# A fused attention and two-layer feed-forward kernel on one core: the second batch's attention result stored unsplit at first, reciprocals parted from their sums, six copies moved from ScalarE to VectorE

## The chip, the cores and the metric

The kernel runs on one core of a Trainium2 chip. The metric is the device time of one execution in microseconds (us). A core has TensorE (PE in the rows; PEld is its weight load), VectorE (DVE), ScalarE (ACT), GpSimd (POOL) and SyncE (SP, which here only starts transfers). Each of them works through its own list of instructions in order; an instruction whose input is not there yet holds up everything behind it on that engine. SBUF is the working memory, PSUM the memory that TensorE writes, in eight banks.

## What is computed

Windowed attention over 2 batches of 8 heads, 768 tokens and 64 features, then two feed-forward layers over all 1536 tokens (512 wide, 2048 hidden), all in float32:

```python
def _attn_ref(q, k, v, n_global, n_local):        # n_global 8, n_local 96
    scores = scale * np.matmul(q, k.transpose(0, 1, 3, 2)) + bias   # bias: -slope[h] * distance
    scores = np.where(keep, scores, -1e9)         # the first 8 keys, and the 96 keys up to the query
    a = np.exp(scores - np.max(scores, axis=-1, keepdims=True))
    a = a / (np.sum(a, axis=-1, keepdims=True) + 1e-09)
    return np.matmul(a, v)
...
x = attention, tokens by (heads * features)
h = x @ w_in;  g = h * np.tanh(log(1 + exp(h)));  x = g @ w_out          # layer 1
h = x @ w_in2; g = relu, or (h + 1) ** 2 / 4 where |h| < 1;  out = g @ w_out2   # layer 2
```

## The kernel before

**Split numbers.** TensorE multiplies in a reduced form of float32 (fp32r). Every operand of the feed-forward layers is therefore kept as two such numbers: a high part, a rounded copy (`rounded`), and a low part, the remainder (`remainder`, value minus high part). `split(hi, lo, src)` makes both, the copy on ScalarE and the subtraction on VectorE. The attention's result is `x_hi` and `x_lo`.

**Attention** is `attention_windows`. It has 24 steps s = 0 to 23: for each batch (0 to 11 the first, 12 to 23 the second) and each of four pairs of heads, t = s mod 3 counts three blocks of 256 queries. In a step, u is the half of the block and j the head of the pair. A step's work is spread over several turns of one loop, so that in turn s each engine gets, in this order:

- TensorE: the scores of step s + 1, the transposes ("turned probabilities") of step s - 2, the product with the values of step s - 3;
- VectorE: `softmax(s, 0)`, two custom instructions that take bias and minimum (L381); `normalise(s-1)`, which adds 1e-9 to the sums (L391, the "total"), takes reciprocals (L392) and leaves the multiplying to GpSimd (L396); the remainders `x_lo` of a finished block (L186); `softmax(s, 1)`; and `evict(s-2, 1)`, the copy of one half of the turned probabilities out of PSUM (tile `pts`, L183);
- ScalarE: the copy `x_hi` of a finished block (L181), the exponentials of step s (L386, each also adds up its row), and between the two pairs of them `evict(s-2, 0)`, the copy of the other half of `pts` (L181).

The scores have two pairs of PSUM banks, so the scores of step s + 1 wait until VectorE has read those of step s - 1; the transposes have one bank for each half, so the transposes of step s - 1 wait for both copies of step s - 2. Steps with t = 0 have 6 blocks of probabilities (copies of 128x384), the others 8 (128x512); the copies of a t = 0 step fall in a turn with t = 2. In turns with t = 2 and t = 0 a finished block of 512 and of 256 tokens is split. A table, `BESIDE`, adds work of the first feed-forward weights (their conversion on all three engines, names such as V00 or T10) and, from step 23 on, the first matmuls of layer 1.

**Layer 1** has steps n = 0 to 31, 16 pieces of the hidden layer for each batch; the second batch's `x_hi` and `x_lo` are read from step 16 on. In step n TensorE makes the hidden piece (L566, L567, L569: 24 matmuls of 384 columns), ScalarE and VectorE make its gate (`ff.gate`: L575 to L605) and convert weights for step n + 2 (among them L186 into `wlo`), and `ff.finish` puts the product with the output weights of step n - 1 on TensorE (L616). A hidden piece of step n + 1 goes into the banks that the gate of step n has to have read (L583). Layer 2 follows, with L625 and, later, L830 and L928 as its matmuls.

The order on every engine is the order in which the code is written: the arm with windows is entered under a manual schedule. The tiles of the weights are `whi` and `wlo`, one pair for each of 16 pieces; those of pieces 14 and 15 are first written late in layer 1.

Of the kernel before, what the change touches and what calls it, by code (L numbers as in the profile page):

```python
# [9 lines left out]
F32 = mybir.dt.float32  # L10
# [6 lines left out]
ALU = mybir.AluOpType  # L17
# [3 lines left out]
P = 128  # L21
# [6 lines left out]
FAR = 2.0 ** 40  # L28
EXP20 = 485165195.40979
PRE, NEAR = 2, 3  # L30

BIAS_ON = "vvappppv"
FIRST_ON = "ppvvvv"
# [14 lines left out]
def attention_then_two_ffn_kernel(  # L48
# [10 lines left out]
    nc = tc.nc  # L59
    B, NP, _, S = q.shape  # L60
    H, D = 2 * NP, P // 2
    NT, DM = out.shape
    NF = w1.shape[0]
# [14 lines left out]
    def half(j):  # L78
        return slice(j * D, (j + 1) * D)
# [48 lines left out]
    halves = [(half(c), slice(PW - c * HQ, P - c * HQ)) for c in range(2)]  # L128
# [35 lines left out]
    for rows, shared in halves:  # L164
        nc.vector.tensor_scalar(dist[rows, shared], rel[rows, shared], ng[rows], nl_far[rows],
                                op0=ALU.is_ge, op1=ALU.add)
# [12 lines left out]
    def rounded(on, to, src):  # L179
        if on == "a":  # L180
            nc.scalar.activation(to, src, AF.Copy)  # L181
        else:
            (nc.vector if on == "v" else nc.gpsimd).tensor_copy(to, src)  # L183

    def remainder(on, to, src, hi):
        (nc.vector if on == "v" else nc.gpsimd).tensor_tensor(to, src, hi.bitcast(F32), op=ALU.subtract)  # L186

    def split(hi, lo, src):
        rounded("a", hi, src)
        remainder("v", lo, src, hi)  # L190
# [122 lines left out]

    SC, TR, PV, HID = ((0, 1), (6, 7)), (2, 3), (4, 5), (6, 7)

    def attention_windows(x_hi, x_lo, bank, wts, opening):
        with ExitStack() as es:
            cp = es.enter_context(tc.tile_pool(name="a_const", bufs=1))
            rp = es.enter_context(tc.tile_pool(name="a_raw", bufs=3))
# [32 lines left out]
            steps = [(b, p, t) for b, p in pairs for t in range(NB // 2)]  # L352
            NU = len(steps)
# [15 lines left out]
                        if not i:  # L369
                            break  # L370

            def softmax(s, u):
                b, p, t = steps[s]
                if u == 0:
                    probs[s] = (prs[s % 3],
                                sp.tile([P, 2, 2, 4], F32, tag="st", name=f"st{s}", bufs=3))
                pr, st = probs[s]
                n = keys(2 * t + u)
                for j, ps in enumerate(scs[s]):
                    h = 2 * p + j  # L380
                    nc.vector.tensor_tensor_reduce(  # L381
                        pr[:, u, j, HQ:HQ + n], ps[:, u, 0:n], bias[:, h, near if n > P else own0],
                        scale=-scale, scalar=3e38, op0=ALU.add, op1=ALU.min,
                        accum_out=st[:, u, j, 0:1],
                    )
                    nc.scalar.activation(pr[:, u, j, HQ:HQ + n], pr[:, u, j, HQ:HQ + n], AF.Exp, scale=-1.0,  # L386
                                         bias=st[:, u, j, 0:1], accum_out=st[:, u, j, 1:2])

            def normalise(s):
                pr, st = probs[s]  # L390
                nc.vector.tensor_scalar(st[..., 2], st[..., 1], 1e-9, None, op0=ALU.add)  # L391
                nc.vector.reciprocal(st[..., 3], st[..., 2])  # L392
                for u in range(2):
                    n = keys(2 * steps[s][2] + u)
                    for j in range(2):
                        nc.gpsimd.tensor_scalar(pr[:, u, j, HQ:HQ + n], pr[:, u, j, HQ:HQ + n], st[:, u, j, 3:4], 1.0,  # L396
                                                op0=ALU.mult, op1=ALU.mult)
# [15 lines left out]
            def evict(s, c):  # L413
                n = len(blocks(s))
                dst, src = pts[s]
                rounded("av"[c], dst[:, 0:n, half(c)], src[c][:, 0:n])

            def values(s):
                b, p, t = steps[s]
                vr = vs[b, p]  # L420
                src = pts.pop(s)[0]
                place = {x: n for n, x in enumerate(blocks(s))}
                for u in range(2):
                    i = 2 * t + u
                    g, (t0, n) = [(g, x) for g, x in enumerate(pieces) if x[0] <= i * P < x[0] + x[1]][0]
                    pv = bank(PV[g], [n])
                    m = key_blocks(i)
                    for o in range(m):
                        for j in range(2):
                            nc.tensor.matmul(pv[half(j), i * P - t0:(i + 1) * P - t0], vr[:, 2 * i - m + 1 + o, j],  # L430
                                             src[:, place[u, j, o]], start=(o == 0), stop=(o == m - 1))
                    if (i + 1) * P == t0 + n:
                        done.append((x_hi[b][:, p, t0:t0 + n], x_lo[b][:, p, t0:t0 + n], pv))

            for h in range(2):
                bias_of(h)
            for s in range(-1, NU + 4):

                if s in (3, 7):
                    wts.load()  # L440
                if s >= 2 and s % 3 == 2 and s // 3 + 3 < len(pairs):
                    load_qk(rp, *pairs[s // 3 + 3])
                if s >= 6 and s % 3 == 0 and s // 3 + 1 < len(pairs):
                    vs[pairs[s // 3 + 1]] = load_v(rp, *pairs[s // 3 + 1])
                ready, done[:] = done[:], []
                for hi, lo, src in ready:
                    rounded("a", hi, src)
                if s + 1 < NU:
                    scores(s + 1)
                if 0 <= s - 2 < NU:  # L450
                    transposes(s - 2)
                if 0 <= s - 3 < NU:
                    values(s - 3)
                if 0 <= s < NU:
                    softmax(s, 0)
                if 0 <= s - 1 < NU:
                    normalise(s - 1)
                for hi, lo, src in ready:
                    remainder("v", lo, src, hi)
                if 0 <= s - 2 < NU:  # L460
                    evict(s - 2, 0)
                if 0 <= s < NU:
                    softmax(s, 1)
                if 0 <= s - 2 < NU:
                    evict(s - 2, 1)
                for name in BESIDE.get(s, ()):
                    opening[name]()
                    if name in ("V01", "V11"):
                        wts.load()


    def attention_all(x_hi, x_lo, bank, wts, opening):
        with ExitStack() as es:
            cp = es.enter_context(tc.tile_pool(name="b_const", bufs=1))
            rp = es.enter_context(tc.tile_pool(name="b_raw", bufs=2))
# [73 lines left out]
            for name in sum((BESIDE[s] for s in sorted(BESIDE)), ()):  # L549
                if name[0] != "b":  # L550
                    opening[name]()
                    if name in ("V01", "V11"):
                        wts.load()


    class FeedForward:
# [453 lines left out]
    def arm(attention, manual):  # L1010
        with ExitStack() as es:
# [26 lines left out]
            opening.update({f"h{n}{i}": lambda n=n: ff.hidden_piece(n) for n in range(2) for i in "ab"})  # L1038
            opening.update({f"g0{i}": lambda: ff.gate_part(0) for i in "abc"})
            batches = [slice(b * S, (b + 1) * S) for b in range(B)]  # L1040
            attention([x_hi[:, :, t] for t in batches], [x_lo[:, :, t] for t in batches], bank, wts, opening)
            wpb = es.enter_context(tc.tile_pool(name="wpb", bufs=1))

            due = {(B - 1) * NF + 2 + (3 * f // 2 if f < 10 else 2 * f - 5): (1, f) for f in range(NF)}

# [3 lines left out]
            def parts_of(n):  # L1049
                if n in due:  # L1050
                    m, f = due[n]
                    return wts.convert(wpa if f < NEAR else wpb, m, f)[1]
                if n + 1 >= NF:
                    return nothing, nothing, wts.finish
                if n + 2 < NF:
                    halves[n + 2] = wts.convert(wpb, 0, n + 2)[2]
                    first_half = halves[n + 2][0]
                else:
                    def first_half(second):
                        second()  # L1060
                _, begin, middle, high = halves[n + 1]
                if n > 1:
                    return begin, middle, lambda: first_half(high)

                def opens():
                    for name in ("R20", "H11", "R11"):
                        opening[name]()
                    begin()

                return opens, middle, lambda: first_half(high)  # L1070

            def again(f, dtype):
                pool = wpa if f < NEAR else wpb
                return [pool.tile([P, 2, DM], dtype, tag=f"w{n}{f}", name=f"w{n}{f}") for n in ("hi", "lo")]

            pair = Pair(x_hi, x_lo, bank, gp, tp, wts, again, dram, ff.finish)
            for n in range(1, ff.count):
                if n > 1:
                    ff.hidden(n)
                ff.gate(n, *parts_of(n))  # L1080
                ff.finish()
                for f in range(4, 12):
                    if n - 2 in due and due[n - 2] == (1, f):
                        pair.save(f)
                if n >= B * NF:
                    pair.beside(n - B * NF)
# [58 lines left out]
```

## Time and profile before

| | |
|---|---|
| median of 3 runs | 600.29 us (598.37 to 601.36) |
| the profiled execution's own time | 597.39 us |
| its span, first to last instruction | 595.6 us |
| TensorE busy | 582.7 us (98%) |
| VectorE busy | 460.0 us (77%) |
| ScalarE busy | 393.9 us (66%) |
| GpSimd busy | 65.2 us (11%) |
| mean granted TensorE clock | 0.999 |

Busy shares are means over the whole span. The attention fills about the first 65 us, layer 1 goes on to about 340 us, layer 2 to the end; each stretch has to be read by itself.

### The profile page before, as it was taken

The page shows a single profiled execution, that of the slowest core. Times are in us where ns is not written, and L with a number is a line of the kernel's source. Part 1 is how long each engine was busy: PE and PEld are TensorE (multiplying, and loading weights), DVE is VectorE, ACT ScalarE, POOL GpSimd, SP SyncE. Part 2 cuts the span into 40 slices and gives each one's busy share as a digit, 9 for nine tenths or more (in the row PEclk, how much of TensorE's full clock was granted, in tenths as well). Part 3 has the DMA queues.
Part 4 walks back from the last instruction along what each step waited for, and adds up shares of the span by engine and source line. Part 5 has one row for each costly group of instructions (what it writes and reads, how often), then busy time and mean ns, then how long its engine had stood idle before and what let it go on. Part 6 is the DMA issues. An engine that isn't in the chain of part 4 may idle for free.

```text
span 595.6 us, 10128 instructions
## 1 busy us (share of the span) xinstructions
PE 582.7 (98%) x3708; PEld 505.6 (85%) x3708; DVE 460.0 (77%) x1038; ACT 393.9 (66%) x872; POOL 65.2 (11%) x156
## 2 busy tenths in 40 slices
PE   5999999999999999999999999999999999999997
PEld 3767889999999999999999988878888888888886
DVE  7999889888888577676776775988788787777572
ACT  5999888888888468676686777577464643543240
POOL 5766600000000000000000000000020140200000
PEclk9999999999999999999999999999999999999999
DMA  7997032344333202241544665600042270310003
GB/s 205 307 297 249 4 134 95 124 142 142 120 103 132 71 1 72 71 142 52 161 139 145 186 205 175 180 32 2 0 137 76 68 216 1 107 36 1 0 18 130
DMA packets 17481, 66.66 MB, mean 112 GB/s; under 512 B 2192, under 2 KB 2704, under 8 KB 13328
## 3 DMA queue, kind: packets, MB, share of 16 engines
q1 hardware_dynamic: 11952, 56.11, 29.6%
q0 software_dynamic: 4608, 8.39, 5.0%
q10 hardware_dynamic: 864, 1.44, 0.6%
q8 instruction: 31, 0.51, 0.4%
q14 instruction: 26, 0.21, 0.1%
HBM read 54.40 MB, written 11.53 MB: 111 GB/s over the span
## 4 chain that ended last, share of the span: by engine, by line
PE 86%; DVE 6%; ACT 6%; issue 1%; POOL 0%; DVEq 0%; POOLq 0%; ACTq 0%
PE psum L616 22%; PE psum L928 15%; PE psum L830 13%; PE psum L566 10%; PE psum L567 10%; PE psum L569 10%; PE psum L625 7%; ACT pr L386 4%; DVE pr L381 1%; ACT pts L181 1%; DVE pts L183 1%; DVE x_lo L186 1%; ACT x_hi L181 0%; DVE wlo L186 0%; PE psum L430 0%
## 5 line engine op out<-in xcount | busy, mean ns | idle before, releaser
L566 PE MATMUL psum<-x_hi,whi 128*128 128x384 f32 (+1 forms) x320 | 111.2, 347 | 0.4 <-DVE kr L583 0.4
L567 PE MATMUL psum<-x_lo,whi 128*128 128x384 f32 (+1 forms) x320 | 110.5, 345 | 0.0
L616 PE MATMUL psum<-g_lo,whi 128*128 128x512 f32 (+1 forms) x256 | 86.7, 338 | 0.1
L616 PE MATMUL psum<-g_hi,wlo 128*128 128x512 f32 (+1 forms) x256 | 86.2, 337 | 0.0
L616 PE MATMUL psum<-g_hi,whi 128*128 128x512 f32 (+1 forms) x256 | 86.1, 336 | 0.0
L569 PE MATMUL psum<-x_hi,wlo 128*128 128x384 f32 (+1 forms) x320 | 71.8, 345 | 0.0
L566 PEld LDWEIGHTS psum<-x_hi,whi 128*128 128x128 f32 x320 | 60.2, 188 | 3.7 <-DVE kr L583 0.6
L181 ACT ACTIVATE whi<-wbits 128x512 fp32r<-128x512 f32 x72 | 44.6, 619 | 27.6 <-DVE wbits L783 14.1
L567 PEld LDWEIGHTS psum<-x_lo,whi 128*128 128x128 f32 x320 | 60.2, 188 | 2.4
L569 PEld LDWEIGHTS psum<-x_hi,wlo 128*128 128x128 f32 x320 | 57.3, 188 | 2.5
L186 DVE TENSOR_TENSOR wlo<-wbits,whi 128x512 fp32r<-128x512 f32 x76 | 51.9, 688 | 9.2 <-ACT whi L181 9.1
L756 POOL DMA_DIRECT2D whi<-kept_hi x16 | 8.7, 541 | 430.9 <-ACT room_lo L869 363.0
L616 PEld LDWEIGHTS psum<-g_lo,whi 128*128 128x128 f32 x256 | 48.2, 188 | 5.8 <-DVE g_lo L605 0.5
L616 PEld LDWEIGHTS psum<-g_hi,whi 128*128 128x128 f32 x256 | 48.2, 188 | 5.7
L616 PEld LDWEIGHTS psum<-g_hi,wlo 128*128 128x128 f32 x256 | 48.1, 188 | 5.7
L238 ACT ACTIVATE wbits<-stage 128x512 uint16<-128x512 uint16 x64 | 50.1, 783 | 0.3 <-DVE wlo L186 0.2
L386 ACT ACTIVATE pr<-pr,st 128x192 f32<-128x192 f32 (+1 forms) x96 | 41.9, 444 | 7.5 <-DVE st L381 7.4
L245 DVE SCALAR_TENSOR_TENSOR wbits<-wsc,wbits 128x512 uint32<-128x512 uint32 x60 | 41.5, 692 | 6.7 <-ACT wbits L238 2.5
L396 POOL TENSOR_SCALAR pr<-pr,st 128x192 f32<-128x192 f32 (+1 forms) x96 | 40.2, 437 | 20.6 <-ACT pr L386 8.2
L173 ACT ACTIVATE wsc<-stage 128x512 f32<-128x512 f32 x60 | 39.6, 660 | 0.0
L367 PE MATMUL psum<-kr,qr 64*64 64x192 f32 (+1 forms) x352 | 25.9, 360 | 8.0 <-DVE wsc L160 5.4
L575 ACT ACTIVATE e<-psum 128x384 f32<-128x384 f32 x32 | 15.5, 487 | 26.0 <-PE psum L569 25.9
(161 smaller groups left out, 1293.3 us busy)
## 6 DMA issues: line engine op xcount, KB each, us to landing
stage<-in_w_dram SPq DMA_DIRECT2D x32, 1024.0 KB, 5.0
vr<-in_v_dram SPq DMA_DIRECT2D x8, 704.0 KB, 10.7
kept_hi<-whi SPq DMA_DIRECT2D x8, 512.0 KB, 7.3
kept_lo<-wlo SPq DMA_DIRECT2D x8, 512.0 KB, 8.0
whi<-kept_hi POOLq DMA_DIRECT2D x16, 256.0 KB, 3.6
wlo<-kept_lo POOLq DMA_DIRECT2D x16, 256.0 KB, 3.7
kr<-in_k_dram SPq DMA_DIRECT2D x14, 216.0 KB, 12.0
qr<-in_q_dram SPq DMA_DIRECT2D x7, 384.0 KB, 11.2
```

The costliest lines, as they stand in the source:

```text
L181: nc.scalar.activation(to, src, AF.Copy)
L186: (nc.vector if on == "v" else nc.gpsimd).tensor_tensor(to, src, hi.bitcast(F32), op=ALU.subtract)
L238: nc.scalar.activation(bits[:, i, :, 0], words(U16, i, 1), AF.Copy, scale=2.0 ** -13, bias=2.0 ** -14 - 0.5)
L245: nc.vector.scalar_tensor_tensor(out[:, i].bitcast(U32), moved(i, U32), 3, out[:, i].bitcast(U32), op0=ALU.logical_shift_left, op1=ALU.bit ...
L386: nc.scalar.activation(pr[:, u, j, HQ:HQ + n], pr[:, u, j, HQ:HQ + n], AF.Exp, scale=-1.0, bias=st[:, u, j, 0:1], accum_out=st[:, u, j, 1:2])
L566: nc.tensor.matmul(ph, wh[:, c], xh[:, c, tok], start=(c == 0), stop=False)
L567: nc.tensor.matmul(ph, wh[:, c], xl[:, c, tok], start=False, stop=False)
L569: nc.tensor.matmul(ph, wl[:, c], xh[:, c, tok], start=False, stop=(c == KD - 1))
L616: nc.tensor.matmul(y, lhs[:, w], rhs[:, t0:t0 + n], start=(f == 0 and i == 0 and c % share == 0), stop=(f == NF - 1 and i == 2 and c % sha ...
L625: nc.tensor.matmul(ys[c], lhs[:, w], rhs, start=(f == 0 and i == 0), stop=(f == NF - 1 and i == 2))
L830: nc.tensor.matmul(ps, a[:, cols], x, start=(n == 0), stop=(n == 3 * HK - 1))
L928: nc.tensor.matmul(ys[c], lhs[:, w], rhs[:, cuts[c]], start=(n == 0 and k == 0), stop=(n == len(fs) - 1 and k == 2))
```

## The change

Three things are edited in `attention_windows`, and one follows in layer 1.

1. *Unsplit result.* For the second batch, a finished block is no longer split. Its 512 tokens are copied to a plain float32 place `raw_x` by ScalarE, its 256 tokens by VectorE. `raw_x` lies in the tiles of weight pieces 14 and 15, which for this come from a pool opened before the attention. The four splits (768 columns each) are done after the gates of layer 1's steps 5, 6, 7 and 8.
2. *Total and reciprocal parted.* `total(s-1)` stays where it was; `normalise(s-1)`, now only the reciprocal and GpSimd's multiplying, moves behind the first instruction of `softmax(s, 1)`, and the remainders move behind it.
3. *Six copies.* For t = 0 steps other than 6 and 9 (0, 3, 12, 15, 18, 21), `evict(s-2, 0)` is done by VectorE in place of ScalarE, and stands right behind the total.

```diff
-            def softmax(s, u):
+            def softmax(s, u, heads=(0, 1)):
...
+            def total(s):
+                st = probs[s][1]
+                nc.vector.tensor_scalar(st[..., 2], st[..., 1], 1e-9, None, op0=ALU.add)
+
             def normalise(s):
                 pr, st = probs[s]
-                nc.vector.tensor_scalar(st[..., 2], st[..., 1], 1e-9, None, op0=ALU.add)
                 nc.vector.reciprocal(st[..., 3], st[..., 2])
...
-                rounded("av"[c], dst[:, 0:n, half(c)], src[c][:, 0:n])
+                on = "v" if steps[s][2] == 0 and s not in (6, 9) else "av"[c]
+                rounded(on, dst[:, 0:n, half(c)], src[c][:, 0:n])
...
-                for hi, lo, src in ready:
-                    rounded("a", hi, src)
+                for g, to, src in ready:
+                    if g != 1:
+                        rounded("a", to[0], src)
...
                     softmax(s, 0)
                 if 0 <= s - 1 < NU:
+                    total(s - 1)
+                if 0 <= s < NU:
+                    if 0 <= s - 2 < NU:
+                        evict(s - 2, 0)
+                    softmax(s, 1, (0,))
+                if 0 <= s - 1 < NU:
                     normalise(s - 1)
-                for hi, lo, src in ready:
-                    remainder("v", lo, src, hi)
-                if 0 <= s - 2 < NU:
+                for g, to, src in ready:
+                    if g is None:
+                        remainder("v", to[1], src, to[0])
+                    elif g == 1:
+                        rounded("v", to[0], src)
+                if 0 <= s < NU:
+                    softmax(s, 1, (1,))
+                elif 0 <= s - 2 < NU:
                     evict(s - 2, 0)
-                if 0 <= s < NU:
-                    softmax(s, 1)
                 if 0 <= s - 2 < NU:
                     evict(s - 2, 1)
...
+        return [lambda p=p: split(x_hi[1][:, p], x_lo[1][:, p], raw_x[p]) for p in range(NP)]
...
                 ff.finish()
+                if n >= LATER and splits:          # LATER = 5
+                    splits.pop(0)()
```

On VectorE, turn 5 of the attention (t = 2) read so before, from the total of step 4 on (`st` holds the sums, ISA is the custom instruction of L381 and the reading of its minimum):

```order
L391 TENSOR_SCALAR st_371<-st_371 128x4
L392 RECIPROCAL st_371<-st_371 128x4
L186 TENSOR_TENSOR x_lo<-psum,x_hi 128x512
L381 ISA pr_190,st_422<-psum,bias 128x192
L381 ISA st_422 128x1
...
L183 COPY pts_401<-psum 128x6x64
```

and reads so in the changed kernel, whose line numbers are its own:

```order
L394 TENSOR_SCALAR st_375<-st_375 128x4
L184 COPY pts_405<-psum 128x6x64
L384 ISA pr_194,st_426<-psum,bias 128x192
L384 ISA st_426 128x1
L398 RECIPROCAL st_375<-st_375 128x4
L187 TENSOR_TENSOR x_lo<-psum,x_hi 128x512
...
L184 COPY pts_405<-psum 128x6x64
```

The first copy of `pts` now stands in front of the softmax of the second half-block, the reciprocal and the remainder behind one half of it; turns 2, 14, 17, 20 and 23 have the same shape, the last three without the remainder. The second place is VectorE in layer 1, between the gates of steps 5 and 6, before (`wlo_7` is weight conversion for step 7, `e` the gate of step 6):

```order
L242 TENSOR_SCALAR wbits<-stage_78 128x512
L245 SCALAR_TENSOR_TENSOR wbits<-wsc,wbits 128x512
L186 TENSOR_TENSOR wlo_7_1842<-wbits,whi_7_1841 128x512
L576 TENSOR_SCALAR e<-e 128x384
L577 SCALAR_TENSOR_TENSOR e<-e 128x384
```

and in the changed kernel:

```order
L243 TENSOR_SCALAR wbits<-stage_78 128x512
L246 SCALAR_TENSOR_TENSOR wbits<-wsc,wbits 128x512
L187 TENSOR_TENSOR wlo_7_1838<-wbits,whi_7_1837 128x512
L187 TENSOR_TENSOR x_lo<-whi_159,x_hi 128x768
L597 TENSOR_SCALAR e<-e 128x384
L598 SCALAR_TENSOR_TENSOR e<-e 128x384
```

One remainder of 768 columns has come in ahead of the next gate, and so it has ahead of the gates of steps 7, 8 and 9. On TensorE, GpSimd and SyncE every instruction stands where it stood.

## Rows read from the trace of the kernel before

**Rows 1.** Busy time by stretch: start:end, length, then busy us of each engine.
```profile
20.00:40.00 20.00, 19.27 (x346) 14.64 (x347) 18.97 (x95) 19.31 (x76) 13.60 (x34) 1.00 1.03 296
40.00:60.00 20.00, 19.05 (x325) 14.18 (x321) 19.42 (x91) 19.08 (x74) 12.98 (x31) 1.00 0.82 246
...
100.00:120.00 20.00, 20.00 (x118) 18.69 (x117) 17.46 (x35) 17.36 (x36) 0.00 (x0) 1.00 0.33 109
```

**Rows 2.** The chain that ended last, in order of time: start, length, what.
```profile
7.72 3.52 ACT pr L386 x16
...
66.26 1.02 PE psum L430 x16
```

**Rows 3.** Timeline of turn 20: start, length, instruction, [idle before <-releaser].
```profile
57.92 0.68 PE L411 MATMUL psum<-ident,pr 64*128 64x64 f32 x12
...
58.39 0.16 DVE L391 TENSOR_SCALAR st<-st 128x4 f32<-128x4 f32 x1
...
58.58 0.18 DVE L392 RECIPROCAL st<-st 128x4 f32<-128x4 f32 x1
...
58.68 0.66 DVE L186 TENSOR_TENSOR x_lo<-psum,x_hi 128x512 fp32r<-128x512 f32 x1
...
59.25 0.35 DVE L381 CUSTOM_DVE_ANT_0 pr<-psum,bias 128x192 f32<-128x192 f32 x1
...
59.80 0.55 DVE L183 COPY pts<-psum 128x384 f32<-128x384 f32 x1
...
60.27 0.28 DVE L381 CUSTOM_DVE_ANT_0 pr<-psum,bias 128x128 f32<-128x128 f32 x1
```

**Rows 4.** Timeline of turn 2 and the start of turn 3.
```profile
11.27 0.37 DVE L391 TENSOR_SCALAR st<-st 128x4 f32<-128x4 f32 x1 [0.28 <-ACT pr L386]
...
11.82 0.59 PE L411 MATMUL psum<-ident,pr 64*128 64x64 f32 x12
...
12.34 0.98 PE L367 MATMUL psum<-kr,qr 64*64 64x192 f32 x16
12.44 0.49 ACT L181 ACTIVATE pts<-psum 128x384 f32<-128x384 f32 x1
...
12.95 0.28 DVE L381 CUSTOM_DVE_ANT_0 pr<-psum,bias 128x128 f32<-128x128 f32 x1
```

**Rows 5.** Timeline of turn 5 and the start of turn 6.
```profile
18.28 0.17 DVE L391 TENSOR_SCALAR st<-st 128x4 f32<-128x4 f32 x1
...
18.32 0.59 PE L411 MATMUL psum<-ident,pr 64*128 64x64 f32 x12
...
19.86 0.51 PE L367 MATMUL psum<-kr,qr 64*64 64x192 f32 x4
```

**Rows 6.** Timeline of turn 21: a total beside a GpSimd instruction.
```profile
60.55 0.68 POOL L177 TENSOR_SCALAR stage<-stage 128x512 f32<-128x512 f32 x1
...
60.69 0.56 DVE L391 TENSOR_SCALAR st<-st 128x4 f32<-128x4 f32 x1
```

**Rows 7.** Timeline of the passage from attention to layer 1.
```profile
78.66 0.58 ACT L181 ACTIVATE x_hi<-psum 128x512 fp32r<-128x512 f32 x1
...
79.27 0.69 DVE L186 TENSOR_TENSOR x_lo<-psum,x_hi 128x512 fp32r<-128x512 f32 x1 [0.39 <-ACT x_hi L181]
...
85.60 0.44 PE L566 MATMUL psum<-x_hi,whi 128*128 128x384 f32 x1 [0.41 <-DVE kr L583]
```

**Rows 8.** Timeline of layer 1, from the end of gate 5 to the hidden piece of step 7.
```profile
122.21 0.69 DVE L186 TENSOR_TENSOR wlo<-wbits,whi 128x512 fp32r<-128x512 f32 x1 [0.70 <-ACT whi L181]
...
122.83 0.35 DVE L576 TENSOR_SCALAR e<-e 128x384 f32<-128x384 f32 x1
...
123.48 0.49 ACT L575 ACTIVATE e<-psum 128x384 f32<-128x384 f32 x1 [0.91 <-PE psum L569]
...
125.96 1.02 DVE L583 SCALAR_TENSOR_TENSOR e<-qr,psum 128x384 f32<-128x384 f32 x2
...
127.47 0.34 PE L566 MATMUL psum<-x_hi,whi 128*128 128x384 f32 x1
```

More of the change, by code (lines that the diff above doesn't have):

```diff
@@ L30 @@
 PRE, NEAR = 2, 3
+LATER = 5
 BIAS_ON = "vvappppv"
@@ L314, in attention_then_two_ffn_kernel, with attention_windows @@
     SC, TR, PV, HID = ((0, 1), (6, 7)), (2, 3), (4, 5), (6, 7)
-    def attention_windows(x_hi, x_lo, bank, wts, opening):
+    def attention_windows(x_hi, x_lo, bank, wts, opening, kept):
+        raw_x = [t.rearrange("p a n -> p (a n)")[:, 0:S] for f in (NF - 2, NF - 1) for t in kept(f, F32)]
         with ExitStack() as es:
@@ L370, in scores @@
                             break
-            def softmax(s, u):
+            def softmax(s, u, heads=(0, 1)):
                 b, p, t = steps[s]
-                if u == 0:
+                if (u, heads[0]) == (0, 0):
                     probs[s] = (prs[s % 3],
@@ L378, in softmax @@
                 n = keys(2 * t + u)
-                for j, ps in enumerate(scs[s]):
-                    h = 2 * p + j
+                for j in heads:
+                    ps, h = scs[s][j], 2 * p + j
                     nc.vector.tensor_tensor_reduce(
@@ L432, in values @@
                     if (i + 1) * P == t0 + n:
-                        done.append((x_hi[b][:, p, t0:t0 + n], x_lo[b][:, p, t0:t0 + n], pv))
+                        tok = slice(t0, t0 + n)
+                        done.append((g if b else None, (raw_x[p][:, tok],) if b else
+                                     (x_hi[b][:, p, tok], x_lo[b][:, p, tok]), pv))
             for h in range(2):
@@ L469, in attention_windows, with attention_all @@
                         wts.load()
-    def attention_all(x_hi, x_lo, bank, wts, opening):
+        return [lambda p=p: split(x_hi[1][:, p], x_lo[1][:, p], raw_x[p]) for p in range(NP)]
+    def attention_all(x_hi, x_lo, bank, wts, opening, kept):
         with ExitStack() as es:
@@ L553, in attention_all @@
                         wts.load()
+        return []
     class FeedForward:
@@ L1040, in arm, with again @@
             batches = [slice(b * S, (b + 1) * S) for b in range(B)]
-            attention([x_hi[:, :, t] for t in batches], [x_lo[:, :, t] for t in batches], bank, wts, opening)
+            pools = {f: wpa for f in (*range(NEAR), NF - 2, NF - 1)}
+            def again(f, dtype):
+                pool = pools[f]
+                return [pool.tile([P, 2, DM], dtype, tag=f"w{n}{f}", name=f"w{n}{f}") for n in ("hi", "lo")]
+            splits = attention([x_hi[:, :, t] for t in batches], [x_lo[:, :, t] for t in batches], bank, wts, opening,
+                               again)
             wpb = es.enter_context(tc.tile_pool(name="wpb", bufs=1))
+            pools.update({f: wpb for f in range(NF) if f not in pools})
             due = {(B - 1) * NF + 2 + (3 * f // 2 if f < 10 else 2 * f - 5): (1, f) for f in range(NF)}
@@ L1051, in parts_of @@
                     m, f = due[n]
-                    return wts.convert(wpa if f < NEAR else wpb, m, f)[1]
+                    return wts.convert(pools[f], m, f)[1]
                 if n + 1 >= NF:
@@ L1055, in parts_of @@
                 if n + 2 < NF:
-                    halves[n + 2] = wts.convert(wpb, 0, n + 2)[2]
+                    halves[n + 2] = wts.convert(pools[n + 2], 0, n + 2)[2]
                     first_half = halves[n + 2][0]
@@ L1070, in parts_of @@
                 return opens, middle, lambda: first_half(high)
-            def again(f, dtype):
-                pool = wpa if f < NEAR else wpb
-                return [pool.tile([P, 2, DM], dtype, tag=f"w{n}{f}", name=f"w{n}{f}") for n in ("hi", "lo")]
             pair = Pair(x_hi, x_lo, bank, gp, tp, wts, again, dram, ff.finish)
```

## The prediction

> **What bounds the kernel now.** First the busy time by stretch [rows 1], to see where the edits fall. Between 20 and 60 us, which is attention, TensorE, VectorE and ScalarE are each busy 19.0 to 19.4 of 20 us: three engines at their limit, none of which can make up more than about 5% of a delay. From 100 to 120 us TensorE is busy all of its 20.00 us while VectorE and ScalarE have 2.5 us of air in 20. The clock is 1.00 in all three stretches, so no edit is paid for or paid back by it. Second, the chain that ended last [rows 2]: it begins on ScalarE's exponentials at 7.72 and is on TensorE from 66.26 us to the end. So a microsecond by which attention hands over later, or earlier, is a microsecond of the result; and behind 66 us only what stops TensorE counts. Third, the timelines of single turns, since in attention the question is which wait ends last.
>
> **VectorE's list in attention.** Turn 20 [rows 3] gives the price of each piece as the distance from start to start, which is what a full engine pays: total to reciprocal 0.19 (58.39 to 58.58), reciprocal to remainder 0.10, remainder of 512 columns 0.57, first softmax piece of the second half-block with its minimum and the second of the same kind 0.55 together (59.25 to 59.80), copy of 384 columns 0.47. The total itself is written after 0.16 us, but the reciprocal behind it starts only 0.19 after it, and it must read what the total wrote; with softmax in between that wait has work in it. I put the parting at -0.1 per turn, between 0 and the whole 0.19.
>
> What the second batch loses: four remainders of 512 columns (0.57 each) become nothing on VectorE, since ScalarE makes the plain copy; four of 256 become copies of 256, at nothing gained or lost. What VectorE gains: six copies of 0.47. For turns 12 to 22 that is 11 x 0.1 + 3 x 0.57 less 3 x 0.47, or 1.4 us less work, and up to 2.0 if the totals that took 0.56 instead of 0.16 [rows 6] become short. ScalarE loses 0.49 per moved copy [rows 4]. By work alone the attention would gain 1.4 to 2.0.
>
> **What the moved copy waits for.** The copy reads transposes, and in VectorE's list it now stands ahead of three softmax pieces, of which TensorE's next scores wait.
>
> - Turn 2 [rows 4]. The total comes at 11.27, the transposes run from 11.82 to 12.41, and ScalarE's copy started at 12.44, the moment they ended. VectorE's copy can't start sooner: it waits about 0.8 us with the rest of its turn behind it. From 12.45: copy 0.47, softmax 0.28, reciprocal 0.10, softmax 0.28, second copy 0.47, so turn 3 begins at about 14.05 where it began at 12.95: +1.1. TensorE's next scores (12.34) need the second half-block read, at about 13.65: +1.3.
> - Turn 5 [rows 5]. TensorE is 1.3 late, so the transposes of 18.32 to 18.91 end at 20.2, while VectorE is ready some 0.3 to 0.8 earlier. From 20.2: copy 0.47, softmax 0.28, reciprocal 0.10, remainder 0.59, softmax 0.28, so the scores of 19.86 start at 22.0: +2.1. I take +2.1 for both turns. Below: if transposes keep pace, as in a turn where they are done before the total, the copy costs only its 0.47 on VectorE and gives 0.49 back on ScalarE: 0 for the two.
> - Turns 6 to 11 have no moved copy. All three engines are full [rows 1], so at most 5% of some 15 us comes back, 0.75; I take 0.2 from the parting.
> - Turns 14, 17, 20, 23. In turn 20 [rows 3] the transposes end at 58.60, the total at 58.55: with the lateness of both engines alike the copy waits almost nothing, but it and the remainder's place now stand ahead of softmax, and TensorE, as full as VectorE, gets its scores later in those turns. A walk in order through these turns with the pitches above gives back nearly all of the 1.4: I take -0.1, with the ends -2.0 (all of VectorE's saving arrives) and +1.0 (a wait of 0.25 in each of the four).
>
> Attention: 2.1 - 0.2 - 0.1 = **+1.8**.
>
> **The passage to layer 1** [rows 7]. The last block's copy of 512 columns on ScalarE (0.58) stays, its remainder on VectorE (0.69, after a wait of 0.39 for that copy) goes. TensorE waits 0.41 at 85.60 for VectorE. **-0.3**, between 0 and -0.41: more than the wait can't be gained there.
>
> **The splits in steps 5 to 8** [rows 8]. Each adds to ScalarE a copy of 768 columns, and to VectorE a remainder of 768. Neither stands in the trace. The copy: by 0.49 for 384 [rows 4] and 0.58 for 512 [rows 7] it is 0.76, at most 1.5 x 0.58 = 0.87; ScalarE has 0.91 of idle time ahead of 123.48, which hides it. The remainder: not under the 0.69 of 512 columns, not over 1.5 x 0.69 = 1.03; by the distance 122.21 to 122.83 it is 1.5 x 0.62 = 0.93, and I take 0.88. So VectorE has 0.88 x 4 = 3.5 us more, against 2.5 us of air in 20 us [rows 1], that is 1.05 in a step of 8.4: the room is there, but in four steps running nearly all of it is used up. Part of that air is the 0.70 for which VectorE waits at 122.21 for ScalarE, and that is moved with the rest rather than filled, since ScalarE in turn waits for VectorE's gate. The first split makes VectorE's L583 of 125.96 some 0.7 late; the bank's first half, read by 126.5, is needed at 127.47, about 0.95 away. Nothing is lost. The three behind it come on top of what the first left over: about 0.3, 0.55 and 0.55. **+1.4**; below it 0 (each step clears its own lateness), above it 2.8 (three splits arrive whole, at 0.93).
>
> **Sum.** 1.8 - 0.3 + 1.4 = +2.9 us. The profiled execution took 597.39, which would make 600.3; it lies 2.9 under the median shown, 600.29, and against that median the time is **603.2 us**. Half a per cent, 3.0 us, is about what a measurement of this kernel can tell from no change; the forecast lies just at that.
>
> **The rivals.**
>
> *Relief on ScalarE carries the attention* (faster). ScalarE starts the chain [rows 2], and loses six copies of 0.49. If the transposes run earlier because ScalarE's exponentials are done earlier, VectorE's copy finds them ready, turns 2 and 5 cost 0, and VectorE's 1.4 to 2.0 comes through. Then 600.29 - 1.7 - 0.3, with the splits at half my price (+0.7): 599.0; with the splits at 0, 598.3, and with ScalarE's relief of 6 x 0.49 on top at most 595.4. It decides if the wait ahead of the copy in turn 2 stays under about 0.3 us. For it: the chain's first link is ScalarE. Against it: at 11.27 VectorE was waiting 0.28 for ScalarE already, and TensorE's transposes began 0.55 behind that [rows 4]. I put this case at **597.8**.
>
> *GpSimd's multiplying meets the totals* (slower). In turn 21 a total of 4 columns took 0.56, starting 0.14 after a GpSimd instruction that ran from 60.55 to 61.23; it ended within 0.02 of that one [rows 6]. In turn 20 the same total took 0.16 [rows 3]. The parted reciprocal is 0.3 to 0.9 us later in its turn, so GpSimd's multiplying by it is later too, and falls on the next turn's total and copies more often. At 0.4 per meeting, and some six more meetings of 24 turns: +2.4, so 603.2 + 2.4 = **605.6**. It decides from about three more meetings on. Against it: the total in turn 5 was short, 0.17 [rows 5], as most are.
> On this the Trainium skill says, in "SBUF — State Buffer", "Who interferes with whom", that VectorE and GpSimd share one port pair under an exclusive lock, held for a whole instruction, the loser blocked. The 0.56 that ends with GpSimd's instruction agrees; by the rule VectorE's copies out of PSUM, with one output in SBUF and no second input there, would be blocked seldom, which speaks for fewer than six meetings.
>
> *The splits are hidden whole*: 603.2 - 1.4 = **601.8**. For it: 0.95 us of slack at the bank against 0.88 of work [rows 8]. Against it: the ring from VectorE to ScalarE and back carries lateness over.
>
> **How the numbers follow.** Forecast 0.42, from 601.7 to 604.7; ScalarE's relief 0.24, from 595.4 to 599; meetings 0.16, from 604.5 to 608; hidden splits 0.18, from 600.5 to 602.5. The limits of no change are 597.3 and 603.3. Faster: a little under half of the second case, 0.10. Slower: about half of the forecast and all of the third, 0.37. No change: the rest, 0.53. The range for 8 in 10 leaves out the far ends of the second and third case: 597.4 to 606.0. The forecast's own is 601.7 to 604.7.
>
> **What the changed profile would show.** VectorE idle before its copy of `pts` in turn 2, for some 0.8 us, released by TensorE's transposes, and turn 3 beginning near 14.05; idle again in turn 5, by 0.3 to 0.8; scores of turn 6 about 2 us late. The same copy in turns 14 to 23 with less than 0.3 of idle time. The first matmul of layer 1 about 1.8 late. No wait of VectorE for an `x_hi` of the second batch, and TensorE's 0.41 at gate 1 shorter. In layer 1 a step 5 as long as step 4, steps 6 to 8 longer by 0.3 to 0.6 with TensorE waiting for L583's successor, and from step 10 on the old length. A remainder of 768 of 0.8 to 1.0. Totals of 0.3 to 0.6 in more than six further turns would be the second rival's mark.
>
> **What would make it wrong.** Above all the turns 12 to 23, where I let waits eat 1.4 us of saved work on the strength of a walk by fixed prices: if TensorE has more air there than 5%, the saving arrives. Then the two waits at the start, whose 2.1 us stand on transposes that don't move: if they move up by 0.5, more than half of it goes. Last, the splits, whose price and whose leftover are both my estimates.

## The result and the profile after

The changed kernel takes **604.87 us** (median of 6 runs, 604.38 to 606.21), the kernel before 600.91 (6 runs, 598.37 to 601.84). The ratio is 1.0074, 95% interval 1.0047 to 1.0101: slower by half a per cent to one. The forecast was 603.2, its range 597.4 to 606.0. Against the kernel before that ran beside it the change costs 4.0 us by the medians, where the sum had 2.9; the likeliest of its three cases, no change (0.53, up to 603.3), did not come, but slower (0.37).

The profiled execution of the changed kernel has a span of 603.5 us, 7.9 more than the 595.6 of the one shown before, twice what the medians differ by. The first view is busy time by stretch (length, busy us of PE, PEld, DVE, ACT, POOL, then granted clock, DMA share, GB/s):

```profile
12.40:19.10 6.70, 5.79 (x64) 4.04 (x64) 4.12 (x22) 3.28 (x14) 3.67 (x9) 0.50 1.02 308
20.00:40.00 20.00, 19.63 (x341) 14.62 (x338) 16.75 (x85) 18.19 (x71) 13.85 (x34) 1.00 1.03 293
100.00:120.00 20.00, 20.00 (x117) 18.96 (x116) 17.01 (x34) 17.30 (x35) 0.00 (x0) 1.00 0.45 151
```

Beside [rows 1] VectorE and ScalarE have lost 2.2 and 1.1 us of busy time between 20 and 40 us: they wait (the changed kernel is 5 us late there, so the same 20 us hold somewhat earlier work). From 100 to 120 us TensorE is full, as before. The first row is new: a granted clock of 0.50, 1.2 GHz, for 6.7 us. The timeline of turns 2 and 3 shows what came ahead of it:

```profile
11.40 0.17 DVE L394 TENSOR_SCALAR st<-st 128x4 f32<-128x4 f32 x1 [0.41 <-ACT pr L389]
...
11.77 1.39 PE L370 MATMUL psum<-kr,qr 64*128 64x128 f32 x12 [2.13 <-DVE st L394]
...
13.10 0.91 PE L417 MATMUL psum<-ident,pr 64*128 64x64 f32 x12
14.03 0.56 DVE L184 COPY pts<-psum 128x384 f32<-128x384 f32 x1 [2.46 <-PE psum L417]
...
14.91 1.90 PE L370 MATMUL psum<-kr,qr 64*64 64x192 f32 x16 [0.92 <-DVE st L384]
```

VectorE stands 2.46 us before the moved copy, from 11.57 to 14.03, with both softmax pieces of the second half-block and the reciprocal behind it; TensorE then waits 0.92 for them. The order of the waits is the predicted one. VectorE's wait is longer because TensorE itself came late, by 2.13 us, at 11.77, and then ran its transposes at the lower clock (0.91 where [rows 4] has 0.59); of TensorE's wait the label says a total of VectorE, but the same wait stands in executions without the change, and the DMA view names the transfer that ends it (`qr` for step 3, issued at 6.96; KB, us to landing):

```profile
qr<-in_q_dram SPq DMA_DIRECT2D x1, 384.0 KB, 4.7
```

It landed at about 11.7, just ahead of the scores. In the profile before the same transfer took 3.7. Turn 5 looks as drawn in the prediction, the lateness apart (timeline):

```profile
22.32 0.17 DVE L394 TENSOR_SCALAR st<-st 128x4 f32<-128x4 f32 x1 [0.23 <-ACT pr L389]
...
22.65 0.58 PE L417 MATMUL psum<-ident,pr 64*128 64x64 f32 x12
23.27 0.56 DVE L184 COPY pts<-psum 128x384 f32<-128x384 f32 x1 [0.77 <-PE psum L417]
...
25.09 0.71 PE L370 MATMUL psum<-kr,qr 64*64 64x192 f32 x11 [0.37 <-DVE st L384]
```

The total is done, the copy waits 0.77 for the transposes, and then TensorE waits 0.37 for what stands behind the copy (in [rows 5] its scores ran on without).

Layer 1, VectorE around the first split and TensorE at the hidden pieces of steps 8, 9 and 10 (timelines):

```profile
128.19 0.69 DVE L187 TENSOR_TENSOR wlo<-wbits,whi 128x512 fp32r<-128x512 f32 x1 [0.70 <-ACT whi L182]
128.93 0.96 DVE L187 TENSOR_TENSOR x_lo<-whi,x_hi 128x768 fp32r<-128x768 f32 x1
129.80 0.35 DVE L597 TENSOR_SCALAR e<-e 128x384 f32<-128x384 f32 x1
```

```profile
91.57 0.44 PE L587 MATMUL psum<-x_hi,whi 128*128 128x384 f32 x1 [0.41 <-DVE kr L604]
...
142.26 0.44 PE L587 MATMUL psum<-x_hi,whi 128*128 128x384 f32 x1 [0.31 <-DVE kr L604]
...
151.28 0.44 PE L587 MATMUL psum<-x_hi,whi 128*128 128x384 f32 x1 [0.38 <-DVE e L604]
...
160.29 0.45 PE L587 MATMUL psum<-x_hi,whi 128*128 128x384 f32 x1 [0.39 <-DVE kr L604]
```

The split leaves the 0.70 wait for ScalarE as it was [rows 8] and adds 0.87 (128.93 to 129.80) behind it. Two steps later TensorE begins to wait: 142.26, 151.28 and 160.29 lie 9.0 apart where hidden pieces lay 8.35 apart before. The wait of 0.41 at gate 1 [rows 7] has not become shorter.

**Where the time went.** Three marks divide the kernel: VectorE's first softmax of turn 6, the first matmul of layer 1, and TensorE's hidden pieces of steps 2 and 14 (us, worked out from the starts in each kernel's trace; the last column is the time from step 2 to step 14 over the 100.34 of before). The medians' differences are to the kernel before on the same chip.

| kernel | turn 6 at | turn 6 to layer 1 | steps 2 to 14 | median, to before |
|---|---|---|---|---|
| before | 20.3 | 46.9 | 0 | |
| after | 25.4 | 47.9 | +1.9 | +4.0 |
| e1 before again | 23.3 | 46.9 | 0 | +0.1 |
| e2 late copies only | 23.6 | 47.9 | +1.9 | +2.5 |
| e3 no copies | 22.3 | 45.7 | +1.9 | +1.1 |
| e4 halves of splits | 27.8 | 46.9 | +1.1 | +5.2 |
| e5 late copies, behind | 22.6 | 46.5 | +1.9 | +1.0 |
| e6 no copies, spaced splits | 22.5 | 45.8 | +0.3 | -1.4 |
| e7 parting alone | 21.8 | 45.8 | 0 | -1.8 |
| e8 all copies, behind | 22.3 | 45.8 | +1.9 | -0.3 |
| e9 parting, two early copies | 24.9 | 47.3 | 0 | +1.9 |
| e10 parting again | 23.7 | 45.9 | 0 | -1.3 |

From the first matmul of layer 1 to step 2 the kernels with unsplit results take 18.2 us, the others 18.3 to 18.4.

### The profile page after: what moved, and what is told of

Same layout as the page of the kernel before. It is cut to its first block, busy times and chain, and to the rows that moved or that the text cites. A ratio compares the mean times of both kernels' runs of the same rounds, so it can differ in the third digit from the quotient of the medians.

```text
span 603.5 us, 10119 instructions
## 1 busy us (share of the span) xinstructions
PE 586.7 (97%) x3708; PEld 506.9 (84%) x3708; DVE 462.6 (77%) x1044; ACT 395.0 (65%) x866; POOL 66.3 (11%) x156
## 4 chain that ended last, share of the span: by engine, by line
PE 88%; DVE 5%; ACT 3%; issue 1%; POOL 1%; DMA 0%; DVEq 0%; ACTq 0%
PE psum L637 18%; PE psum L949 14%; PE psum L851 13%; PE psum L587 9%; PE psum L588 9%; PE psum L590 9%; PE psum L646 7%; PE psum L437 3%; PE psum L370 3%; PE psum L417 2%; ACT pr L389 1%; DVE x_lo L187 1%; DVE g_lo L626 1%; DVE kr L598 1%; POOL pr L402 1%
```

## Experiments

**e1: before again.** No edit.

> The kernel before, unchanged, to see what part of the 7.9 us between the two profiled executions (595.6 and 603.5) belongs to the change, when the medians lie only 4.0 apart. In the execution of the changed kernel that was profiled, TensorE waited 2.13 us ahead of the scores at 11.74, and its clock was 0.50 from 12.4 to 19.1 us. Theory (the start varies from execution to execution): this profile differs from the one of before in the first 20 us, by about 2 to 3 us, and its span is 597 to 600. Rival (all of it comes from the change): softmax of turn 6 starts at 20.4 as before, the span is 595.6 to 596.5.

Measured: 600.36 against 600.22, ratio 0.9995 (0.9974 to 1.0016). Its profiled span is 598.7, and 3.0 of the 3.1 us over the profile before lie ahead of turn 6. So of the 5.1 by which the changed kernel's profile reached turn 6 late, some 3 belong to chance, and times of single profiles are compared from turn 6 on only.

**e2: late copies only. e3: no copies.**

```diff
-    on = "v" if steps[s][2] == 0 and s not in (6, 9) else "av"[c]
+    on = "v" if steps[s][2] == 0 and s not in (0, 3, 6, 9) else "av"[c]    # e2
+    on = "av"[c]                                                           # e3
```

> The changed kernel with the first two of the six copies (steps 0 and 3, turns 2 and 5) back on ScalarE. Theory (VectorE's copies wait for transposes in turns 2 and 5): the 2.1 us of these two turns come back, 604.9 becomes 602.5 to 603.2, and turn 6 starts within 0.5 us of the kernel before. Rival (the late start is that of the transfers and the clock, by chance of the execution): no change, 604.5 to 605.2.

Measured: 602.70, ratio 1.0041 (1.0024 to 1.0058), 2.2 under the changed kernel, 1.5 when each is taken against the kernel before that ran with it: the theory's price, or somewhat less. Turn 6 comes within 0.3 of e1, not of the profile before.

> The changed kernel with all six copies back on ScalarE; the parting, the unsplit result and the splits in steps 5 to 8 stay. By the price of VectorE's work in the second batch (11 x 0.1 + 3 x 0.57 us less) attention would be 1 to 2 us shorter than before, the splits cost 1.9 as in the trace of the changed kernel: 600.0 to 601.8, level with before. If the four late copies pay as well (relief on ScalarE), this is 1 us or more slower than the run with only those four; if they cost, it is 1 us or more faster.

Measured: 601.28, ratio 1.0011 (0.9993 to 1.0029). Without the four late copies it is 1.4 faster, and the stretch to layer 1 shrinks from 47.9 to 45.7. The copies cost, the relief on ScalarE pays nothing. In e2, turn 14, VectorE waits 0.44 before the copy, and TensorE stands for 1.15 us soon after; in e9, an experiment below with no moved copy in that turn, it stands as long in the same place (timelines, e2 and then e9):

```profile
45.98 0.56 DVE L184 COPY pts<-psum 128x384 f32<-128x384 f32 x1 [0.44 <-PE psum L417]
48.12 0.38 PE L437 MATMUL psum<-pts,vr 128*64 128x128 f32 x2 [1.15 <-issue]
```

```profile
49.57 0.27 PE L433 MATMUL psum<-pts,vr 128*64 128x128 f32 x1 [1.14 <-issue]
```

Both stands fall inside one product with the values, and "issue" means that the profile shows nothing that ended them. So TensorE's 1.15 can't be put down to the copy, as I did when I wrote down what I expected of e5. The length of the turn can: from VectorE's first softmax of turn 14 to that of turn 15 it takes 3.6 us in e3, e6, e7, e9 and e10, which have no copy on VectorE there, and 4.2 to 4.6 in the changed kernel, e2 and e4, which have it ahead of softmax.

**e4: halves of splits.**

```diff
-LATER = 5
+LATER = 2
-        return [lambda p=p: split(x_hi[1][:, p], x_lo[1][:, p], raw_x[p]) for p in range(NP)]
+        return [lambda p=p, w=w: split(x_hi[1][:, p, w], x_lo[1][:, p, w], raw_x[p][:, w])
+                for p in range(NP) for w in (slice(0, S // 2), slice(S // 2, S))]
```

> The changed kernel with each split cut in two halves of 384 columns, eight of them after steps 2 to 9 in place of four after steps 5 to 8. In the trace of the changed kernel each whole split made its step 0.46 to 0.67 us longer, and ScalarE caught up 0.33 us in each step without one. Theory (ring of VectorE and ScalarE with a gain of 0.33 per step): half a split costs about 0.37, of which 0.33 is made up in the step itself; steps 3 to 10 stay at 8.35 to 8.45 and 1.5 to 1.9 us come back: 603.0 to 603.4. Rival (each split costs TensorE in proportion to its work, wherever it stands): eight halves cost as much as four wholes, 604.5 to 605.2.

Measured: 605.38, ratio 1.0081 (1.0050 to 1.0111), which by the median is the rival. The trace says otherwise: the splits cost 1.06 instead of 1.90, nothing up to the hidden piece of step 6, 0.5 at step 8 and 0.11 to 0.16 in each of the four behind. The profiled execution lost it again ahead of turn 6, where its `qr` landed 6.2 us after its issue; one execution's late transfer doesn't explain a median, and what took the gain back in the six runs (603.54 to 608.68) is not shown. So the theory's direction is borne out in layer 1 of one trace alone, and its 0.4 at most was too little.

**e5: late copies behind softmax. e8: all six behind.** The copy of those turns is written after both pieces of `softmax(s, 1)`, in e5 on the kernel of e2, in e8 on the changed kernel:

```diff
-                    if 0 <= s - 2 < NU:
+                    if 0 <= s - 2 < NU and not (s >= 12 and s % 3 == 2):   # e8: not s in (2, 5, 14, 17, 20, 23)
                         evict(s - 2, 0)
...
                     softmax(s, 1, (1,))
+                    if s >= 12 and s % 3 == 2:                             # e8: the same six
+                        evict(s - 2, 0)
```

> The four late copies on VectorE as in the run with late copies only, but each written behind both softmax pieces of the second half-block instead of ahead of them. In that run VectorE stood 0.44 us before the copy at 45.98 while TensorE waited 1.15 us for the scores; with no copy on VectorE at all, VectorE waits 3.3 us for ScalarE between 20 and 66 us. Theory (the place costs, not the work): the stretch from the softmax of turn 6 to the first matmul of layer 1 falls from 47.9 to 45.7 or less (before: 46.9), the median to 600.3 to 601.3. Rival (1.9 us more work on a full VectorE cost whatever their place): the stretch stays above 47, the median at 602 to 603.

Measured: 601.07, ratio 1.0016 (1.0001 to 1.0031); the stretch is 46.5, between the two theories. By the medians, each against the kernel before on its chip, the place is worth 1.4 of e2's 2.5, and what is left, 1.0, is what e3 has with no copy at all (1.1). In turn 14 the copy still costs VectorE time, 4.1 us against 3.6, but by the medians it does not reach the result.

> All six copies stay on VectorE, but behind both softmax pieces of the second half-block, the two early ones (turns 2 and 5) too. Late copies only, ahead: 602.7; late copies only, behind: 601.1; all six ahead: 604.9. Theory (an early copy costs because softmax stands behind its wait for the transposes): the two early copies cost nothing in this place, the median is 600.8 to 601.6, the level of the four late ones behind. Rival (the early ones cost as work on VectorE, or what ScalarE no longer does there): 602.5 to 603.5, two more than that.

Measured: 600.68, ratio 1.0001 (0.9978 to 1.0024), against e5's 1.0016: the two early copies cost nothing that shows when softmax doesn't stand behind their wait.

**e6: spaced splits**, on e3.

```diff
-LATER = 5
+LATER = 2
-                if n >= LATER and splits:
+                if n >= LATER and (n - LATER) % 3 == 0 and splits:
```

> All six copies on ScalarE, and the four splits after steps 2, 5, 8 and 11 instead of 5, 6, 7 and 8. In layer 1 four splits in a row cost 1.90 us, eight halves in a row 1.06, and the first ones cost TensorE nothing. Theory (a stock of slack that each step without a split fills by 0.33 us): after a split of 0.7 two free steps suffice, TensorE's steps stay at 8.35 throughout, and 1.9 us come back from the run without copies: 599.2 to 599.8, faster than before by about 0.1 to 0.2%. Rival (each whole split costs about 0.5 wherever it stands): 601.0 to 601.6 again.

Measured: 598.65, ratio 0.9981 (0.9958 to 1.0003). That is better than the theory's bracket. From step 2 to step 14 it loses 0.26 where four splits in a row lost 1.90. Between 70 and 180 us TensorE has one wait left, the 0.4 at gate 1 that stands in the kernel before too (view of waits: what waited, us in total, times, longest):

```profile
PE psum L587 <- DVE kr L604: 0.4, 1, 0.4
```

**e7: parting alone, and e10, the same again.** The kernel before with edit 2 of the change and nothing else; the copies, the split results and layer 1 are those of before.

```diff
...
                 if 0 <= s - 1 < NU:
+                    total(s - 1)
+                if 0 <= s < NU:
+                    if 0 <= s - 2 < NU:
+                        evict(s - 2, 0)
+                    softmax(s, 1, (0,))
+                if 0 <= s - 1 < NU:
                     normalise(s - 1)
                 for hi, lo, src in ready:
                     remainder("v", lo, src, hi)
-                if 0 <= s - 2 < NU:
+                if 0 <= s < NU:
+                    softmax(s, 1, (1,))
+                elif 0 <= s - 2 < NU:
                     evict(s - 2, 0)
-                if 0 <= s < NU:
-                    softmax(s, 1)
...
```

> The kernel before with the total and the reciprocal parted (and the remainders behind the first piece of softmax) and nothing else. Without copies on VectorE the changed kernel passed from the softmax of turn 6 to layer 1 in 45.7 us against 46.9; either the parting or the unsplit result did that. Theory (the unsplit result, 0.57 us of VectorE's work in each of turns 14, 17 and 20): the stretch of the parting alone is 46.5 to 46.9, the median 599.8 to 600.3. Rival (the parting, 0.1 in each turn or more with what GpSimd held up): 45.7 to 46.1, median 599.0 to 599.5.

Measured: 598.22, ratio 0.9977 (0.9956 to 0.9998), stretch 45.8: the rival, with a time below its bracket. The parting alone gives the whole 1.1, all of it from turn 12 on (turns 6 to 11 take 16.2 us in both), and the unsplit result (e3, 45.7) adds 0.1.

> The parting alone once more, since it is the fastest of all so far (598.22 against 600.03, interval of the ratio 0.9956 to 0.9998). If it is a gain of its own: 597.8 to 598.8, with the stretch from the softmax of turn 6 to layer 1 again 45.7 to 46.0 us against 46.9. If the gain was one of a lucky start: 599.5 to 600.5, and a stretch above 46.5.

Measured: 599.66, ratio 0.9972 (0.9951 to 0.9994), stretch 45.9. The time by itself falls into the second bracket, but the kernel before was slower on this chip too (601.0); by ratio and stretch it is a gain of its own. It is the lowest ratio of all versions, though e6's interval overlaps with it.

**e9: the parting and the two early copies**, ahead of softmax, on e7.

```diff
-                rounded("av"[c], dst[:, 0:n, half(c)], src[c][:, 0:n])
+                rounded("v" if s in (0, 3) else "av"[c], dst[:, 0:n, half(c)], src[c][:, 0:n])
```

> The kernel with the parting alone, and of the six copies only the first two (steps 0 and 3) on VectorE ahead of softmax. In medians the two cost 2.2 when the late four were there too (604.9 against 602.7). Theory (two waits of their own, independent of the rest): 598.2 + 2.2, or 600.0 to 601.2. Rival (the loss at the start comes back later, as in attention the engines take up an early delay): 598.0 to 599.0.

Measured: 602.85, ratio 1.0036 (1.0013 to 1.0060), 3.2 over e10 on the same chip: the theory, with 1.0 more than its price. Its profile has the two waits, 2.48 us in turn 2 and 0.78 in turn 5:

```profile
13.88 0.56 DVE L183 COPY pts<-psum 128x384 f32<-128x384 f32 x1 [2.48 <-PE psum L414]
...
22.78 0.56 DVE L183 COPY pts<-psum 128x384 f32<-128x384 f32 x1 [0.78 <-PE psum L414]
```

## Why the prediction held, and where its steps were off

- **Turns 2 and 5, +2.1.** Right in kind, and in size as far as the runs can tell: 1.5 to 2.2 between the medians of the changed kernel and e2, 3.2 between e9 and e10. e8 shows the cause: same work, other place, no cost. The wait in turn 5 was 0.77 (forecast 0.3 to 0.8), and with the copy ahead of softmax that turn takes 4.0 us (the changed kernel, e4, e9) against 2.6 to 3.2 in all other profiles. The wait in turn 2 was 2.46, not 0.8, because I read it from an execution in which the `qr` transfer landed early; without the copy VectorE stands somewhere in that time too (1.64 in e1, 3.12 in e10, before its own copy of that turn), so the price stayed near 2.
- **Turns 6 to 23, -0.3.** The step that failed: measured +1.0, of which 0.1 falls in turns 6 to 11 (forecast -0.2) and 0.9 behind them (forecast -0.1). "The copy waits almost nothing" was wrong: in turns 14, 17, 20 and 23 it waited 0.11, 0.08, 0.40 and 0.40, on average the 0.25 that I had put down for the upper end of +1.0. The saved work did not arrive either. I counted three dropped remainders in turns 12 to 22, but only turns 17 and 20 drop one; the remainder in turn 14 is the first batch's. Those two turns are indeed 0.6 shorter in e3 than in e7 (1.7 and 1.8 us against 2.3 and 2.4), and the turn behind each is 0.6 longer, where VectorE waits for ScalarE's sums (timeline of e3):

```profile
54.08 0.27 DVE L394 TENSOR_SCALAR st<-st 128x4 f32<-128x4 f32 x1 [0.45 <-ACT pr L389]
...
61.67 0.72 DVE L394 TENSOR_SCALAR st<-st 128x4 f32<-128x4 f32 x1 [0.63 <-ACT pr L389]
```

By parts: the parting -1.1 (e7), the unsplit result -0.1 (e3 less e7), the late copies +2.2 (changed kernel less e3), but +1.1 with e4, which has the same attention, and +1.4 by medians (e2 less e3). So the size of the miss is open between 0.2, by e4's 46.9, and 1.3; 0.6 of it is turn 22 of the changed kernel's profile, 2.9 us long where e2 and e4 take 2.3, with a total of 0.91 beside GpSimd.
- **The passage, -0.3.** The 0.2 fell between the first matmul and step 2; the wait at gate 1, from which I took it, stayed 0.41. The cause I gave is not the one.
- **The splits, +1.4.** Right mechanism, term too small: +1.9, in the hidden pieces of steps 8 to 11. The remainder of 768 took 0.96, the copy 0.83; VectorE's distance of 0.87 was my 0.88. Against my 0, 0.3, 0.55 and 0.55 the four splits cost 0, 0.46, 0.67 and 0.66, and 0.11 came after them. Too small was what each split leaves to the next. e6 shows that this leftover, and not the work, is the price.
- **The rivals.** ScalarE's relief: no, e3 is faster than e2. Meetings with GpSimd: no; totals over 0.25 us are 6 of 24 in both traces. All twelve end within 0.03 us of the end of a GpSimd instruction. The lock rule of the Trainium skill ("SBUF — State Buffer", "Who interferes with whom") fits them, but with as many before as after it did not decide the result. Splits hidden whole: no as written, nearly so when spaced.
- **The sum.** 604.87 is 1.7 above the forecast, inside the range but above the forecast's own band (to 604.7): 0.6 of that is the kernel before, 600.91 in six runs instead of 600.29, and 1.1 the terms, 4.0 by the medians instead of 2.9. By the traces they come to 3.8 with e4's turns 6 to 23 and to 4.8 with the changed kernel's own. The two large terms, early copies and splits, had the predicted causes. Where the middle term comes out near its -0.3, as in e4, that is luck: waits and savings were both misjudged.

**Open.** Kernels with the same instructions from turn 6 on differ up to layer 1: e9 and e10 take 47.3 and 45.9 us, the changed kernel and e4 47.9 and 46.9, e5 and e8 46.5 and 45.8. In e9 TensorE stands 0.99 us at 41.21 and 1.14 at 49.57, both without a releaser in the profile, in e10 in neither place, and five of the turns from 12 on are longer; what chooses between the two was not tried. So differences below about 1.4 us in that column rest on the medians.

## What to carry to other kernels

Before moving a copy to another engine, look at what its input waits for and at what stands behind it in the new list: here the same six copies cost about 3 us ahead of softmax and nothing that the medians show behind it. Work put into an engine's slack is free only if the steps between have time to fill the slack again: four splits in a row cost 1.9 us, the same four every third step 0.3. When a change has several parts, run each alone: one small part, the parting, was worth -0.2 to -0.3%, and the rest hid it.

## What the runs showed that was not expected

The start varies from execution to execution: the `qr` transfer of step 3 landed 3.7 us after its issue in the profile before and 4.2 to 6.2 in the eleven others. Turn 6 came at 24.9 to 27.8 us with the early copies ahead of softmax and at 20.3 to 23.7 in all other profiles. The profile on which the prediction rested was the luckiest.

TensorE's clock belongs to that start. It fell to 0.50 from 12.4 to 19.1 us in the changed kernel's profile, after TensorE had stood idle for 2.13 us: sixteen transposes took 1.12 us (16.74) and 0.71 when the clock was back (20.07). The kernel before did the same in e1 (timelines of the changed kernel and of e1):

```profile
16.74 1.12 PE L417 MATMUL psum<-ident,pr 64*128 64x64 f32 x16
```

```profile
15.40 1.12 PE L411 MATMUL psum<-ident,pr 64*128 64x64 f32 x16
```

In e1 the view of stretches reads 1.00 there, because its trace holds no clock record ahead of 18.2 us. The matmuls show the same in e2, e4, e6, e9 and e10; e3, e5 and e8 have a recorded 0.50 for some 3.4 us, and the profile before and e7 none. In e7 TensorE had stood idle for 2.08 us and yet twelve transposes took 0.59, so idle time alone does not decide it. A mean clock near 1.000 therefore doesn't tell whether an execution had this, and how much of the start's delay is the clock's is not shown. The price of the early copies doesn't rest on it: turn 5 of the changed kernel, all of it at full clock, has its own waits of 0.77 and 0.37.
